# Block sums of w_out by transfers, and an earlier transpose of tokens, in a fused attention and feed-forward kernel

## The chip, the cores and the metric

The kernel runs on one core of one Trainium2 chip. The metric is the device time of one execution in microseconds; the time before is the median of three runs. A core has five engines with queues of their own: TensorE (PE; its weight loads are listed as PEld), VectorE (DVE), ScalarE (ACT), GpSimd (POOL) and SyncE (SP, which only issues transfers here). Transfers (DMA) are issued from an engine's queue and carried by 16 DMA engines. An engine works through its instructions in program order; one that waits holds up all that stand behind it.

## What is computed

There are two stages. For each of 8 batches and 8 heads, tokens `x` (512 x 64) and states (32 x 64) read one another by softmax attention. The 544 resulting rows of each batch, with 512 features, go through a feed-forward network with a leaky ReLU. Inputs and output are float32.

```python
B, H, S, Ns, D = (8, 8, 512, 32, 64)
scores = scale * np.matmul(x, state.transpose(0, 1, 3, 2))
a = softmax(scores)                       # over the 32 states
xread = np.matmul(a, state)
scores2 = scale * np.matmul(state, x.transpose(0, 1, 3, 2))
a2 = softmax(scores2)                     # over the 512 tokens
sread = np.matmul(a2, x)
rows = concatenate([xread, sread])        # (B * 544) x 512
h = rows @ w_in                           # 512 -> 2048
out = np.maximum(0.01 * h, h) @ w_out     # 2048 -> 512
```

(`softmax` and `rows` stand here for the few lines that the reference has in their place.)

## The kernel before

**Stages of a batch.** The 512 tokens of a batch are cast from `xl` (float32, one buffer) to `xb` (bf16, four buffers) and transposed to `xT` (two buffers). TensorE makes the scores `sc` from `xT` and the transposed states `st_t` (line 205). VectorE and ScalarE turn them into the probabilities `aT` (tokens over states) and `a2` (states over tokens). The product of states and `w_in` is made first, as `M` (line 326), so that the first layer of the tokens is one product of `M` and `aT` (line 347); ScalarE writes it through the leaky ReLU to `hT`. `a2` is transposed to `a2T`, and the states' reads `psr` (line 299) are made from `a2T` and `xb`; their feed-forward comes at the very end, for all batches together.

**Second layer.** Batches 0 and 1 go through `w_out` directly (`piece`, line 375). From batch 2 on, the product of `hT` and `w_out` is made by a scheme of the Strassen-Winograd kind: `hT` is seen as 2 x 2 blocks A, `w_out` as 2 x 2 blocks B11, B12, B21, B22, and seven block products are made in place of eight (class `Fast`; class `Batch` for tokens). The scheme needs four sums of blocks of A for each batch (`Fast.sums`, line 434, VectorE) and, once for the whole kernel, four sums of blocks of B, the tiles `tw[0]` to `tw[3]` (128 x 8 x 256 bf16, 512 KB each, in the buffers `xf0`, `xf1`, `x10` and `x11` that held early inputs). VectorE makes the sums of B in `weights_sum` (line 411), in batch 2. Product 6 uses `tw[1]`, 5 uses `tw[0]`, 7 uses `tw[2]`, and 4 uses `tw[3]`; they run in the order 1, 2, 6, 5, 7, 3, 4 as `units` of eight slices each. The outputs of a batch are put together by `join` (line 457, VectorE) and one addition on GpSimd (line 515), and stored in two transfers of 512 KB from SyncE (line 482).

**Order.** The order of instructions on every engine is the order of the program, written out by hand. Batch 1 and each batch from 2 on runs a loop of 16 steps `s`; a step makes one slice of the first layer and fills in slices of the second layer. In batch `b` the loop also prepares batches `b + 1` and `b + 2`:

- step 0: `load_x(b + 2)` (SyncE; it waits for the casts that read `xl` before) and the transpose `a2T` of batch `b` (SyncE)
- step 1: scores of batch `b + 1`, which need its `xT`; four casts of batch `b + 2` on GpSimd (line 105), which wait for `xl` and for the buffer of `xb` that batch `b - 2` had
- steps 3 and 8, batch 2 only: the sums of B; also in batch 2, the states' reads of batches 0, 1 and 2 in steps 4, 6 and 8, the load of the states of batches 4 to 7 (step 4) and their cast on GpSimd and transpose `st_t` (step 8)
- step 11: the transpose `xT` of batch `b + 2` on SyncE (`a_xt_dma`, line 189)

From batch 3 on, the second layer of the batch before is finished within this loop, and its two output transfers are put into SyncE's queue around steps 9 and 11, ahead of the transpose of step 11.

Of the kernel before, what the change touches and what calls it, by code (L numbers as in the profile page):

```python
# [10 lines left out]
B, H, S, D = 8, 8, 512, 64  # L11
# [16 lines left out]
def kernel(  # L28
# [240 lines left out]
    def a_exp2(a, g):  # L269
        if g == 0:  # L270
            a.e2 = att.tile([P, 2, S], BF16, name="e2", tag="e2")
            a.r2 = att.tile([P, 2], FP32, name="r2", tag="r2")
        nc.scalar.activation(  # L273
            out=a.e2[:, g], in_=a.sc[:, g, :], func=AF.Exp,
            bias=a.m2s[:, g:g + 1], scale=SCALE, accum_out=a.r2[:, g:g + 1],
        )
# [124 lines left out]
    def weights_open():  # L401
        for tag in ("xf0", "xf1", "x10", "x11"):
            tw.append(consts.tile([P, NM, HC], BF16, name=f"tw_{tag}", tag=tag))

    def weights_sum(dst):
        u, v, op = (
            (B12, B11, ALU.subtract), (B11, tw[2], ALU.subtract),
            (B22, B12, ALU.add), (tw[1], B21, ALU.add),
        )[dst]
        with nc.allow_low_precision(reason="operands of a product"):  # L410
            nc.vector.tensor_tensor(out=tw[dst][:], in0=u[:], in1=v[:], op=op)

    class Fast:

# [8 lines left out]
        def sums(self, n, m0=0, m1=NM, eng=None):  # L423
            A, S = self.A, self.S
            if n not in S:
                pool, tag, bufs = self.homes[n]
                S[n] = pool.tile([P, NM, self.q], BF16, name=f"su{n}", tag=tag, bufs=bufs)
            u, v, op = (
                (A[2, 1], A[2, 2], ALU.subtract), (S[0], A[1, 1], ALU.subtract),
                (A[2, 1], A[1, 1], ALU.subtract), (A[1, 2], S.get(1), ALU.add),  # L430
            )[n]
            ms = slice(m0, m1)
            with nc.allow_low_precision(reason="operands of a product"):
                (eng or nc.vector).tensor_tensor(out=S[n][:, ms], in0=u[:, ms], in1=v[:, ms], op=op)  # L434
# [19 lines left out]
            copy(t[:], bank)  # L454

        def join(self, dst, bank, n):
            nc.vector.tensor_tensor(out=dst, in0=bank, in1=self.sv[n][:], op=ALU.add)  # L457

    def rows_of(b):
        return out[b * SROW:b * SROW + S, :].rearrange("(p t) f -> t p f", t=NT)  # L460
# [2 lines left out]
    class Batch:  # L463
# [42 lines left out]
        def done(self, n, bank):  # L506
            f = self.f
            if n in (1, 6, 5, 7):
                f.save(n, bank)
            if n == 2:  # L510
                f.join(self.yo(0)[:, :, :HC], bank, 1)
                if self.b == B - 1:
                    self.out(0, slice(0, HC))
            elif n == 7:
                nc.gpsimd.tensor_tensor(  # L515
                    out=self.yo(1)[:, :, HC:], in0=f.sv[7][:], in1=f.sv[5][:], op=ALU.add
                )
                if self.b == B - 1:
                    self.out(1, slice(HC, DM), eng=nc.scalar)
            elif n == 3:  # L520
                f.join(self.yo(0)[:, :, HC:], bank, 6)
                self.out(0, slice(HC if self.b == B - 1 else 0, DM))
            elif n == 4:
                f.join(self.yo(1)[:, :, :HC], bank, 7)
                self.out(1)
# [257 lines left out]
    for s in range(16):  # L783
        ff1(a1, h1, s)
        if s % 2:
            pb, hT, i, jq = fill[s // 2]
            piece(pb, hT, i, jq, copy=VEC if s == 3 else SCA)
        if s == 4:
            a_scores(a2)
            m_evict(a2, 0, a_m(a2, 0, "big"), SCA)  # L790
            a_shift(a2)
            a_max2(a2)
        elif s == 7:
            a_exp(a2)
            a_open(att_of[3], 3)
            a_xt_dma(att_of[3])
        elif s in (9, 11):
            a_exp2(a2, s // 2 - 4)
            if s == 9:
                a_probs(a2)  # L800
            else:
                a_probs2(a2)
        elif s == 13:
            a_probs2(a1)
            a_a2t(a1)
            pm = [a_m(a2, 1, "big"), a_m(a2, 2, "sc")]
            m_evict(a2, 1, pm[0], VEC)
            m_evict(a2, 2, pm[1], SCA)
# [1 line left out]


    before = None
    weights_open()
    for b in range(2, B):
        hT = hpool.tile([P, 16, S], BF16, name="hT", tag="hT")
        a = att_of[b]
        nxt = att_of[b + 1] if b + 1 < B else None
        now = Batch(b, hT)
        std = []
        if b == 2:  # L820
            std = [(i, 3) for i in range(2)] + [(i, jq) for i in range(2, NT) for jq in range(4)]

        def fill(s):
            n = (PACE2 if b == 2 else PACE)[s]
            left = min(n, len(before.units)) if before else 0
            if left:
                before.run(left)
            if n > left:
                now.run(n - left)

        for s in range(16):
            if s == 11:
                fill(s)
            ff1(a, hT, s)
            if s == 0:
                if b + 2 < B:
                    load_x(b + 2, nc.sync)
                    open_xb(b + 2)
                a_a2t(a)
                if before:  # L840
                    for n in (0, 1):
                        before.f.sums(n, 4, 8)
            elif s == 1:
                if nxt is not None:
                    a_scores(nxt)
                m_evict(a, 3, a_m(a, 3, "big"), SCA)
                if nxt is not None:
                    a_shift(nxt)
                if b + 2 < B:
                    for h in range(0, H, 2):  # L850
                        cast_x(b + 2, h, h + 2, POO)
                if before:
                    before.f.sums(2, 4, 8)
            elif s == 3:
                if before:
                    before.f.sums(3)
                if nxt is not None:
                    a_max2(nxt)
                if b == 2:
                    weights_sum(0)  # L860
                    weights_sum(2)
            elif s == 4:
                if b == 2:
                    load_state(1)
                    a_sread(a0)
            elif s == 6:
                if b == 2:
                    a_sread(a1)
            elif s == 8:
                a_sread(a)  # L870
                if b == 2:
                    state_t(1)
                    weights_sum(1)
                    weights_sum(3)
            elif s == 11 and b + 2 < B:
                a_open(att_of[b + 2], b + 2)
                a_xt_dma(att_of[b + 2])
            elif s == 12:
                for n in range(3):
                    now.f.sums(n, 0, 4)  # L880
            if nxt is not None:
                if s == 5:
                    a_exp(nxt)
                elif s in (7, 8):
                    a_exp2(nxt, s - 7)
                    if s == 7:
                        a_probs(nxt)
                elif s == 11:
                    a_probs2(nxt)
                elif s in (12, 13):  # L890
                    SCA(nxt.M[:, s - 12, DM:2 * DM], pm1[:, s - 12, :])
            if std:
                i, jq = std.pop(0)
                piece(1, h1, i, jq)
            elif s != 11:
                fill(s)
            if s == 10 and nxt is not None:
                pm0 = a_m(nxt, 0, "big")
                pm1 = a_m(nxt, 1, "sc")
                pm2 = a_m(nxt, 2, "ph")  # L900
                for g, copy in enumerate((VEC, SCA)):
                    copy(nxt.M[:, g, 2 * DM:3 * DM], pm2[g][:])
                m_evict(nxt, 0, pm0, SCA)
        before = now
# [31 lines left out]
    for n, more in ((1, 2), (2, 2), (6, 1), (5, 1), (7, 1), (3, 0), (4, 0)):  # L936
        bank = v if n in (2, 5, 3) else u
        for m in range(NM):
            fs.unit(bank, n, m, first=n in (1, 2, 5, 4))
        if n in (1, 6, 5, 7):  # L940
            fs.save(n, bank)
        if n == 2:
            fs.join(ysb[0][:, :, :HC], bank, 1)
        elif n == 7:
            nc.gpsimd.tensor_tensor(
                out=ysb[1][:, :, HC:], in0=fs.sv[7][:], in1=fs.sv[5][:], op=ALU.add
            )
        elif n == 3:
            fs.join(ysb[0][:, :, HC:], bank, 6)
            out_s(0)  # L950
        elif n == 4:
            fs.join(ysb[1][:, :, :HC], bank, 7)
            out_s(1)
        before.run(more)
# [39 lines left out]
```

## Time and profile before

| | us |
|---|---|
| three runs | 211.01, 209.01, 211.02 (median 211.01) |
| profiled execution, its own time | 210.52 |
| its span | 208.7 |
| busy: TensorE, VectorE, ScalarE, GpSimd | 196.6, 144.3, 143.6, 41.4 |
| VectorE, four sums of B (line 411) | 1.21, 1.63, 1.22, 1.51 |
| transpose of tokens, issue to landing (6 of them) | 4.4 to 6.8, median 5.1 |
| transpose of `a2`, issue to landing (8) | 3.1 to 8.8, median 5.2 |
| load of `xl` from SyncE, 1 MB, issue to landing (5) | median 6.4 |

The span is that of the profiled instructions; the execution's own time has another 1.8 us around it. Times in the profile are microseconds from the start of the span. The profile names a tile by its name in the program without its number, so the four `tw` tiles appear as `tw_xf` (`tw[0]`, `tw[1]`) and `tw_x` (`tw[2]`, `tw[3]`), and the sums of A as `su`. The granted clock of TensorE is full throughout.

### The profile page before, as it was taken

The numbers are of one execution on the slowest core, as the hardware profiler recorded it, in microseconds if no ns is written. First come the engines' busy times: TensorE is split into PE (matmuls) and PEld (weight loads), VectorE is DVE, ScalarE is ACT, GpSimd is POOL, SyncE is SP. The second block draws the span as 40 slices with busy tenths as digits, with TensorE's granted clock in tenths as the row PEclk, the third lists the DMA queues.
The fourth block names the chain that finished last, engine by engine and source line by source line (L and its number), as shares of the span: only waits on it lengthen the run. The fifth ranks groups of instructions, "written<-read, shape, count | busy, mean of one in ns | idle before, by whom it ended". The sixth has DMA issues, their size and how long they took to land.

```text
span 208.7 us, 4393 instructions
## 1 busy us (share of the span) xinstructions
PE 196.6 (94%) x1779; PEld 126.4 (61%) x1804; DVE 144.3 (69%) x217; ACT 143.6 (69%) x276; POOL 41.4 (20%) x64
## 2 busy tenths in 40 slices
PE   6789999999999999999999999978999999999990
PEld 2443534443455567766776677645777677788880
DVE  1777589699699969976996699657966702462331
ACT  2459748688969897977797869765878864666210
POOL 8831002040053106200350054000020002000070
PEclk9999999999999999999999999999999999999999
DMA  5999993997655394059904960391025002210035
GB/s 177 229 207 285 220 268 93 208 302 146 182 156 168 96 243 91 3 201 201 155 0 180 229 152 0 137 194 27 0 104 151 0 3 100 100 53 0 3 84 167
DMA packets 38772, 27.74 MB, mean 133 GB/s; under 512 B 24352, under 2 KB 35744, under 8 KB 38752
## 3 DMA queue, kind: packets, MB, share of 16 engines
q1 hardware_dynamic: 33280, 20.39, 38.2%
q0 software_dynamic: 4912, 6.55, 15.3%
q10 hardware_dynamic: 560, 0.52, 1.0%
q8 instruction: 14, 0.23, 0.5%
q14 instruction: 6, 0.05, 0.1%
HBM read 17.30 MB, written 8.91 MB: 126 GB/s over the span
## 4 chain that ended last, share of the span: by engine, by line
PE 84%; DMA 6%; DVE 5%; ACT 2%; issue 1%; ACTq 0%
PE yq L445 34%; PE ph L347 20%; PE py L375 9%; PE pm L326 4%; PE ph L358 3%; PE pyw L375 3%; DMA xT<-xb 3%; DMA xf<-in_x_dram 2%; PE psr L299 2%; PE ph L691 2%; PE yu L445 2%; PE yv L445 1%; PE sc L205 1%; PE php L691 1%; DVE su L434 1%
## 5 line engine op out<-in xcount | busy, mean ns | idle before, releaser
L352 ACT ACTIVATE hT<-ph 128x512 bf16<-128x512 f32 x112 | 65.7, 603 | 22.5 <-PE ph L347 18.7
L347 PE MATMUL ph<-aT,M 128*128 128x512 bf16 x208 | 61.9, 379 | 0.8 <-ACT hT L352 0.5
L445 PEld LDWEIGHTS <-su 128*128 128x128 bf16 x416 | 39.9, 98 | 13.8 <-DVE su L434 1.2
L445 PEld LDWEIGHTS <-hT 128*128 128x128 bf16 x288 | 27.8, 98 | 12.7 <-issue 2.1
L105 POOL CAST xb<-xl 128x512 bf16<-128x512 f32 (+1 forms) x21 | 18.3, 910 | 62.8 <-DMA xl<-in_x_dram 49.5
L347 PEld LDWEIGHTS <-M 128*128 128x128 bf16 x224 | 21.7, 98 | 10.9 <-issue 1.7
L445 PE MATMUL yq<-tw_xf,su 128*128 128x256 bf16 x192 | 27.5, 273 | 0.3
L445 PE MATMUL yq<-w_out_bf,hT 128*128 128x256 bf16 x192 | 27.0, 273 | 0.1
L434 DVE TENSOR_TENSOR su<-hT 128x1024 bf16<-128x1024 bf16 x24 | 16.9, 705 | 11.0 <-ACT hT L352 11.0
L375 PE MATMUL py<-w_out_bf,hT 128*128 128x512 bf16 x91 | 23.4, 379 | 0.2
L375 PEld LDWEIGHTS <-hT 128*128 128x128 bf16 x128 | 11.9, 98 | 14.3 <-issue 1.3
L457 DVE TENSOR_TENSOR yo<-yq,sv 128x512 f32<-128x512 f32 x17 | 11.7, 685 | 11.6 <-PE yq L445 11.6
L515 POOL TENSOR_TENSOR yo<-sv,sv 128x512 f32<-128x512 f32 x6 | 7.6, 1268 | 47.6 <-ACT sv L454 43.7
L454 ACT COPY sv<-yq 128x512 f32<-128x512 f32 x24 | 14.0, 584 | 2.1 <-PE yq L445 1.4
L340 ACT CAST M<-pm 128x1024 bf16<-128x1024 f32 x13 | 13.2, 1014 | 2.9 <-PE pm L326 2.8
L445 PE MATMUL yq<-tw_x,su 128*128 128x256 bf16 x96 | 13.9, 273 | 0.0
L445 PE MATMUL yq<-w_out_bf,su 128*128 128x256 bf16 x96 | 13.1, 273 | 0.0
L445 PE MATMUL yq<-tw_x,hT 128*128 128x256 bf16 x88 | 12.1, 273 | 0.0
L215 DVE TRANSPOSE_TENSOR_REDUCE mrow<-sc 128x32 f32<-128x1024 f32 x7 | 8.7, 1245 | 4.1 <-PE sc L205 4.0
L273 ACT ACTIVATE e<-sc,mcols 128x512 bf16<-128x512 f32 x16 | 11.0, 693 | 0.1
L265 DVE TENSOR_REDUCE mcol<-sc 128x2 f32<-128x1024 f32 x8 | 9.7, 1214 | 0.0
L358 PE MATMUL ph<-sr_t,w_in_bf 128*128 128x256 bf16 x64 | 9.6, 273 | 0.0
(131 smaller groups left out, 256.1 us busy)
## 6 DMA issues: line engine op xcount, KB each, us to landing
xl<-in_x_dram SPq DMA_DIRECT2D x5, 1024.0 KB, 6.4
out_dram<-yo SPq DMA_DIRECT2D x10, 512.0 KB, 2.7
w_in_bf<-in_moe_w_in_dram POOLq DMA_DIRECT2D x4, 512.0 KB, 9.5
w_out_bf<-in_moe_w_out_dram POOLq DMA_DIRECT2D x4, 512.0 KB, 16.8
out_dram<-ysb SPq DMA_DIRECT2D x8, 256.0 KB, 4.6
xf<-in_x_dram SPq DMA_DIRECT2D x2, 512.0 KB, 5.4
x<-in_x_dram POOLq DMA_DIRECT2D x2, 512.0 KB, 13.6
xl<-in_x_dram POOLq DMA_DIRECT2D x1, 1024.0 KB, 18.6
```

The source lines that it names most:

```text
L105: copy(xs[b][:, :, h0:h1].rearrange("p t h d -> p h t d"), xl[b][:, h0:h1].rearrange("p h (t d) -> p h t d", t=NT),)
L265: nc.vector.tensor_reduce(out=m2[:], in_=a.sc[:], axis=AX.X, op=ALU.max, negate=True)
L273: nc.scalar.activation(out=a.e2[:, g], in_=a.sc[:, g, :], func=AF.Exp, bias=a.m2s[:, g:g + 1], scale=SCALE, accum_out=a.r2[:, g:g + 1],)
L340: copy(a.M[:, :, cols], pm[:])
L347: nc.tensor.matmul(ph[:], lhsT=a.M[:, g, P * j:P * (j + 1)], rhs=a.aT[:, g, :], start=(g == 0), stop=(g == 1),)
L352: nc.scalar.activation(out=hT[:, j, :], in_=ph[:], func=AF.Prelu, alpha=0.01)
L358: nc.tensor.matmul(ph[:, :n], lhsT=w_in_bf[:, k, P * j:P * (j + 1)], rhs=sr_t[:, k, :], start=(k == 0), stop=(k == NK - 1),)
L375: nc.tensor.matmul(y.py, lhsT=hT[:, j, P * i:P * (i + 1)], rhs=w_out_bf[:, j, :], start=(j == 0), stop=(j == 15),)
L434: (eng or nc.vector).tensor_tensor(out=S[n][:, ms], in0=u[:, ms], in1=v[:, ms], op=op)
L445: nc.tensor.matmul(bank[:, i, :], lhsT=lhs[:, m, P * i:P * (i + 1)], rhs=rhs[:, m, :], start=(first and m == 0 and (i == 0 or of is not No ...
L454: copy(t[:], bank)
L457: nc.vector.tensor_tensor(out=dst, in0=bank, in1=self.sv[n][:], op=ALU.add)
```

## The change

Three things are changed together.

The sums of B are made by transfers. In step 9 of the loop of batch 1, four plain transfers in SyncE's queue copy B11, B11, B12 and B21 into `tw[0]` to `tw[3]`. In batch 2, four transfers in GpSimd's queue add to them: `tw[2]` += B22 and `tw[0]` += B12 in step 0, `tw[1]` += `tw[2]` in step 3, and `tw[3]` += `tw[1]` in step 8. In program order on GpSimd, the first two stand ahead of the casts of step 1, the third behind these, and the fourth behind the cast of states of step 8. VectorE makes none.

Since a transfer only adds, signs change: `tw[0]` is B12 + B11 where it was B12 - B11, and `tw[1]` is B11 + B22 + B12 where it was B11 - (B22 + B12). The sum of A number 2 is negated, and product 6 (as saved in `sv[6]`) and the addition on GpSimd are subtracted where they were added.

The transpose of tokens for batch `b + 2` is issued in step 7 in place of step 11 from batch 3 on; in batch 2 it stays in step 11.

```diff
         for tag in ("xf0", "xf1", "x10", "x11"):
             tw.append(consts.tile([P, NM, HC], BF16, name=f"tw_{tag}", tag=tag))
+            nc.sync.dma_start(tw[-1][:], (B11, B11, B12, B21)[len(tw) - 1])
+
     def weights_sum(dst):
-        u, v, op = (
-            (B12, B11, ALU.subtract), (B11, tw[2], ALU.subtract),
-            (B22, B12, ALU.add), (tw[1], B21, ALU.add),
-        )[dst]
-        with nc.allow_low_precision(reason="operands of a product"):
-            nc.vector.tensor_tensor(out=tw[dst][:], in0=u[:], in1=v[:], op=op)
+        nc.gpsimd.dma_start(tw[dst][:], (B12, tw[2][:], B22, tw[1][:])[dst], accum_op=ALU.add)
...
-                (A[2, 1], A[1, 1], ALU.subtract), (A[1, 2], S.get(1), ALU.add),
+                (A[1, 1], A[2, 1], ALU.subtract), (A[1, 2], S.get(1), ALU.add),
...
         def join(self, dst, bank, n):
-            nc.vector.tensor_tensor(out=dst, in0=bank, in1=self.sv[n][:], op=ALU.add)
+            op = ALU.subtract if n == 6 else ALU.add
+            nc.vector.tensor_tensor(out=dst, in0=bank, in1=self.sv[n][:], op=op)
...
-                    out=self.yo(1)[:, :, HC:], in0=f.sv[7][:], in1=f.sv[5][:], op=ALU.add
+                    out=self.yo(1)[:, :, HC:], in0=f.sv[5][:], in1=f.sv[7][:], op=ALU.subtract
...
         elif s in (9, 11):
+            if s == 9:
+                weights_open()
...
-    weights_open()
     for b in range(2, B):
...
                 a_a2t(a)
+                if b == 2:
+                    weights_sum(2)
+                    weights_sum(0)
...
                 if b == 2:
-                    weights_sum(0)
-                    weights_sum(2)
+                    weights_sum(1)
...
                     state_t(1)
-                    weights_sum(1)
                     weights_sum(3)
-            elif s == 11 and b + 2 < B:
-                a_open(att_of[b + 2], b + 2)
-                a_xt_dma(att_of[b + 2])
...
+            if s == (11 if b == 2 else 7) and b + 2 < B:
+                a_open(att_of[b + 2], b + 2)
+                a_xt_dma(att_of[b + 2])
```

The addition in the states' own feed-forward at the end (line 946) is changed to a subtraction in the same way.

More of the change, by code (lines that the diff above doesn't have):

```diff
@@ L945 @@
             nc.gpsimd.tensor_tensor(
-                out=ysb[1][:, :, HC:], in0=fs.sv[7][:], in1=fs.sv[5][:], op=ALU.add
+                out=ysb[1][:, :, HC:], in0=fs.sv[5][:], in1=fs.sv[7][:], op=ALU.subtract
             )
```

## The prediction

> **What bounds the kernel now.** I read the page's engine totals and slices first, then the waits, the chain of waits, and the instructions in order of time on SyncE's queue, TensorE, GpSimd and VectorE.
>
> ```profile
> PE 196.6 (94%) x1779; PEld 126.4 (61%) x1804; DVE 144.3 (69%) x217; ACT 143.6 (69%) x276; POOL 41.4 (20%) x64
> PE   6789999999999999999999999978999999999990
> ```
>
> TensorE is busy for 196.6 of 208.7 us and has 12.1 us left. The second line (40 slices of 5.2 us) shows where: the start, the last slice, and one dip at slices 26 and 27. VectorE has 31% to spare, so taking work from it helps only where TensorE waits for it.
>
> ```profile
> PE sc L205 <- DMA xT<-xb: 2.2, 1, 2.2
> ```
>
> In TensorE's own waits (us in all, times, longest) the dip is one wait of 2.2 us, for a transpose of tokens; the next longest, 1.2 us, is at the start. In the chain of waits the same place reads (start, us, what):
>
> ```profile
> 134.84 6.84 DMA xT<-xb
> ...
> 141.72 0.41 PE sc L205 x8
> ```
>
> This is the transpose for batch 7, issued in step 11 of batch 5. Earlier ones land after 5.1 us, at 91.94 + 5.1 = 97.0 and 113.22 + 5.1 = 118.3, and their scores run at 97.13 and 118.31: nearly no slack there either. They are issued late because SyncE's queue goes in order and stands behind two output transfers that wait for `yo`. The median of three runs is 211.01 us with one run at 209.01; one such stall could be that difference, which a single trace can't show.
>
> Now SyncE's queue around the block sums (start, us):
>
> ```profile
> 46.70 2.67 SPq L189 DMA_TRANSPOSE xT<-xb  x1
> 52.33 1.23 SPq L291 DMA_TRANSPOSE a2T<-a  x1
> 53.61 0.57 SPq L99 DMA_DIRECT2D xl<-in_x_dram  x1
> 59.75 1.24 SPq L291 DMA_TRANSPOSE a2T<-a  x1
> ...
> 70.53 2.81 SPq L189 DMA_TRANSPOSE xT<-xb  x1
> ```
>
> and who needs them on TensorE:
>
> ```profile
> 65.20 0.63 PE L299 MATMUL psr<-a2T,xb 128*128 128x64 bf16 x16
> ...
> 75.99 0.41 PE L205 MATMUL sc<-xT,st_t 64*32 64x512 bf16 x8
> ...
> 76.55 1.05 PE L445 MATMUL yq<-tw_xf,su 128*128 128x256 bf16 x8
> ```
>
> The `a2T` issued at 59.75 lands after 3.1 us at 62.85 and is needed at 65.20: 2.35 us of slack. The `xT` issued at 70.53 lands after 5.2 us at 75.7 and is needed at 75.99: 0.3 us. The first use of a block sum is 76.55 (`tw[1]`), then `tw[2]` at 81.78 and `tw[3]` at 87.47.
>
> **The transpose moved to step 7 (batches 3 to 5).** It goes ahead of both output transfers. It then waits only for GpSimd's casts: in batch 5 these end at 122.62 + 3.74 = 126.4, so even with the slow landing of 6.84 it is there at 133.2, for a need at 139.5. On the queue it takes 3.5 us, to 129.9; the output behind it starts at 131.05, so nothing is pushed. In batch 3 the casts end at 83.6 and the output comes at 88.85: again clear. The next `xl` and `a2T` go out earlier. Worth 2.2 us, the whole stall; bounds 0 (a run without it) and 2.2. In batch 2 nothing moves.
>
> **VectorE's sums taken away.** 1.21 + 1.63 + 1.22 + 1.51 = 5.57 us, at 60.5 to 63.2 and 66.9 to 69.7. TensorE waits for VectorE nowhere between 56 and 76, so zero; it can't lose, and at most about 0.4 us of small waits on `su` later could go. GpSimd's four casts beside them took 4.34 us, against 3.14 in batch 4; I take 3.3. The three changed signs cost nothing: the same instruction with another operation.
>
> **Four plain transfers (step 9 of the batch-1 loop).** They wait for nothing recent and go out behind the `xT` of 46.70, from 49.4, 0.5 us each, done before the `a2T` of 52.33. Each moves 512 KB in pieces of 512 bytes. The trace has no such transfer, but rows on both sides of that size (window, share of the engines' time, GB/s at the end):
>
> ```profile
> 56.00:58.00 2.00, 2.00 (x11) 0.88 (x9) 1.93 (x3) 1.40 (x4) 0.00 (x0) 1.00 1.03 368
> 73.00:75.00 2.00, 2.00 (x16) 1.36 (x14) 0.47 (x2) 1.96 (x4) 0.00 (x0) 1.00 1.12 207
> 25.00:26.00 1.00, 1.00 (x13) 0.71 (x11) 0.52 (x1) 0.00 (x0) 0.00 (x0) 1.00 1.22 204
> ```
>
> The first is `xl` in 1 KB pieces, the second transposes within SBUF in smaller ones, the third the converting loads that GpSimd issued. So 1.4 us (368) to 2.5 us (207) each; by pieces, 1 KB takes 1024 x 16 / 368 = 45 ns on one engine, and half of it 23 to 25 ns, 64 pieces per engine: 1.6 us. I take that, 6.4 in all. The engines are free from 50.7 (the `xT` done) and now stay busy to 57.1.
>
> **Four adding transfers (GpSimd's queue).** One reads two blocks and writes one. Low end 1.4 us, a plain copy; high end 104 ns a piece, the mean of GpSimd's queue (15.3% of 16 engines' span over 4912 packets), 6.7 us. I take two reads of 512 bytes as one piece of 1 KB, 45 ns, 3 us; the converting loads' 204 GB/s gives 2.5. GpSimd issues one in 0.8 to 0.9 us, as it did its loads. The first waits for the third plain transfer, which lands at about 50.7 + 4.8 + 0.8 = 56.3; both are out at 58, and GpSimd had nothing to do before 59.94, so this wait alone blocks nobody. But their 6 us of traffic meets SyncE's.
>
> That meeting is the price. At 57.1 SyncE's queue still owes `a2T` (1.4 us of the engines' time, 0.71 of the 2 us from 53) and `xl` (3.2 us, the shares from 55 to 59 added), then the second `a2T` (1.4). How SyncE's transfers fare beside a full queue of GpSimd's, the DMA issues show (KB each, us to landing):
>
> ```profile
> stf<-in_state_dram SPq DMA_DIRECT2D x8, 32.0 KB, 2.2
> ...
> stf<-in_state_dram SPq DMA_DIRECT2D x8, 16.0 KB, 6.2
> ```
>
> Small loads of states landed after 6.2 us at the start, between GpSimd's weight loads, and twice as large ones after 2.2 us later, without them. So SyncE's queue has no precedence, and I let the two share evenly. The first `a2T` is through at 58.5 and lands near 59.5, needed at 62.15: no wait. `xl` takes 2 x 3.2 us and ends at 64.9 in place of 58.6; the `a2T` behind it has the rest of the adds beside it, ends near 67.4 and lands near 68.3. Needed at 65.20: **TensorE waits 3.1 us**.
>
> The Trainium skill ("DMA: Bandwidth & Descriptors", Why small descriptors are slow (HBM only)) says that transfers within SBUF are spared what small pieces cost, and its section Where 436 GB/s comes from lets them run at 435 GB/s, 1.2 us a plain transfer. By that page, an estimate, the adds begin at 57 and the second `a2T` lands near 65.5, the wait shrinks to 0.3 us and the time to 209.1. The transposes within SBUF at 207 GB/s above speak against it; it counts with the rival in which nothing is late.
>
> What else is late: casts from 65.6 to 68.9 in place of 64.3; then, new in GpSimd's order, the third add (0.9 us), so the cast of states ends at 70.9 in place of 68.6; the transpose of states (68.65 before), an output and `xT` follow at about 72.8, landing at 78, 2.0 us after 75.99. TensorE is by then 3.1 us late already, so this lies inside it. The third add, issued at 69.8, lands at about 75.5, before 76.55 + 3.1; the fourth waits for it on GpSimd, whose next work is at 79.86, and lands by 81 for 87.47.
>
> Sum: 210.52 (the profiled execution: span 208.7 and 1.8 around it) - 2.2 + 3.1 = 211.4. The median lies 0.5 above that execution: **211.9 us**.
>
> **The rivals.** *Nothing is late.* The adds run at 1.4 us, or SyncE's queue is hardly slowed: without sharing, `xl` ends at 61.7 and `a2T` lands at 64.0, within its slack, and the casts end at 66, so `st_t` and `xT` slip by under 0.5 us. For it: all engines are idle from 51 to 53 and near 59 to 60. Against: three transfers in a row have to stay on time with 0.3 us left on the last. Time: 210.5 - 2.2 + 0.5 = 208.8.
>
> *The adds are slow, and the change ends slower.* At 6.7 us each, with plain ones at 2.5, the first two adds keep the engines to about 74; `xl` ends at 68 to 70, `a2T` lands at 72 to 73, 7.5 us after 65.20. The third add, which waits for the first and stands behind the casts, lands near 82 for a need at 76.55, 5.5 us, inside the same delay. Time: 210.5 - 2.2 + 7.5 + 0.5 = 216.3. Between the forecast (3 us an add, a wait of 3.1) and this, the wait passes 4.3 us, the gain of 2.2 and 1% of the time besides, at about 4 us an add: there it decides. For it: 104 ns is what that queue showed; against: that was beside the whole start-up load.
>
> *The early transpose doesn't do it*, because SyncE waits for late casts at step 7. It would give back the 2.2 us, 211 with nothing late and 214 with the wait of 3.1. The casts end 13 us before the need in batch 5, so it has no chance of its own.
>
> **How the numbers follow.** About 1% is what a measurement of this kernel can tell from no change: 208.9 to 213.1. Forecast (wait of 1.5 to 5 us, 210.3 to 213.8): 0.45, of which 0.27 within 1% and 0.18 above. Nothing late: 0.30, of which 0.27 faster by over 1% (208.8 is just that) and 0.03 not quite. Slow adds: 0.25, all slower. Together 0.27 faster, 0.30 within, 0.43 slower. The forecast's own range is 210.3 to 213.8; one that holds 8 in 10 has to take in both rivals, 208.8 and 216.3, each with a few tenths for the median's spread: 208.4 to 216.5.
>
> **What would show it.** In TensorE's waits, `sc <- xT` of batch 6 is gone, and a wait `psr <- a2T` of some 3 us stands near 65, in batch 2. The plain transfers land in 1.6 us steps from 52 to 58; the adds last 3 us; GpSimd's casts of batch 2 start near 65.6. Wrong if the casts still start at 60, if a wait for `tw` shows at 76, or if stalls appear in batches 3 to 5.

## The result and the profile after

The changed kernel takes 223.06 us (median of 4 runs, 220.55 to 223.80), the kernel before 210.91 beside it: a ratio of 1.056 (95% interval 1.049 to 1.063). Medians here and below are of all runs, while ratios leave out those over 1.5% above the fastest of their kernel (213.31 us of the kernel before, 222.93 of `adds_states_early`, and 342.8 of `both_early`, at a granted clock of 0.56). The change makes the kernel slower by 12 us; the forecast was 211.9, the top of its range 216.5. The profiled execution took 220.55 us with a span of 218.8, 10.1 more than before. The page's totals and the granted clock in 40 slices (5.5 us each):

```profile
PE 199.6 (91%) x1779; PEld 127.3 (58%) x1804; DVE 137.6 (63%) x213; ACT 144.0 (66%) x276; POOL 41.0 (19%) x68
PEclk9999999999998579999999999999999999999999
```

VectorE is 6.7 us less busy, and no gain from it shows. TensorE is 3 us busier with the same instructions; its clock fell in slices 12 to 14, counted from 0. Its longest waits (us in all, times, longest):

```profile
PE psr L299 <- DMA a2T<-a: 7.9, 1, 7.9
PE sc L205 <- DMA xT<-xb: 1.7, 2, 1.3
```

The 2.2 us for `xT` in batch 6 are gone, as forecast. The wait of `psr` for `a2T` is where it was forecast, near 65, and 7.9 us long in place of 3.1. In the chain of waits (start, us, what) a second transfer follows it:

```profile
59.90 13.42 DMA a2T<-a
...
82.15 6.38 DMA xT<-xb
88.53 0.04 issue
88.57 0.41 PE sc L205 x8
```

The scores of batch 4 start at 88.57, at 75.99 before: 12.6 us late. From there on nothing more is lost; the span is 10.1 longer, which is 12.6 less the 2.2 of batch 6 and a few tenths. So these scores are the place that counts, and both transfers in the chain come late. SyncE's queue (start, us to issue):

```profile
49.82 1.41 SPq L406 DMA_DIRECT2D tw_xf<-w_out_bf  x2
51.33 2.87 SPq L406 DMA_DIRECT2D tw_x<-w_out_bf  x2
54.29 3.60 SPq L291 DMA_TRANSPOSE a2T<-a  x1
57.94 1.50 SPq L99 DMA_DIRECT2D xl<-in_x_dram  x1
59.90 5.76 SPq L291 DMA_TRANSPOSE a2T<-a  x1
...
67.08 8.44 SPq L169 DMA_DIRECT2D stf<-in_state_dram  x8
...
79.49 1.19 SPq L176 DMA_TRANSPOSE st_t<-stb  x1
...
82.15 4.50 SPq L189 DMA_TRANSPOSE xT<-xb  x1
```

and GpSimd (start, us, idle before and what ended it):

```profile
57.80 1.58 POOL L409 DMA_DIRECT2D tw_x<-w_out_bf  x1 [11.01 <-DMA tw_x<-w_out_bf]
58.71 2.27 POOL L409 DMA_DIRECT2D tw_xf<-w_out_bf  x1
69.74 2.29 POOL L105 CAST xb<-xl 128x512 bf16<-128x512 f32 x4 [8.77 <-DMA xl<-in_x_dram]
71.97 0.86 POOL L409 DMA_DIRECT2D tw_xf<-tw_x  x1
78.84 0.62 POOL L175 CAST stb<-stf 128x512 bf16<-128x512 f32 x1 [6.01 <-DMA out_dram<-ysb]
```

The issues themselves have become long while the transfers' engines are full: the eight small loads of states take 8.4 us to issue, where before, with the cast that needs them, they read:

```profile
62.15 3.86 SPq L169 DMA_DIRECT2D stf<-in_state_dram  x8
...
67.53 1.10 POOL L175 CAST stb<-stf 128x512 bf16<-128x512 f32 x1 [3.24 <-DMA stf<-in_state_dram]
```

The adds land after 10.2, 14.3, 6.0 and 6.4 us, the plain transfers after 3.6 to some 8.5. The casts, forecast for 65.6, start at 69.7, and the cast of states at 78.8 where it was at 67.5.

### The profile page after: what moved, and what is told of

Same layout as the page of the kernel before. It is cut to its first block, busy times and chain, and to the rows that moved or that the text cites. A ratio compares the mean times of both kernels' runs of the same rounds, so it can differ in the third digit from the quotient of the medians.

```text
span 218.8 us, 4403 instructions
## 1 busy us (share of the span) xinstructions
PE 199.6 (91%) x1779; PEld 127.3 (58%) x1804; DVE 137.6 (63%) x213; ACT 144.0 (66%) x276; POOL 41.0 (19%) x68
## 4 chain that ended last, share of the span: by engine, by line
PE 65%; DMA 25%; DVE 3%; POOL 2%; issue 1%; ACT 1%; SPq 0%; POOLq 0%; ACTq 0%
PE yq L443 32%; PE ph L347 17%; DMA xl<-in_x_dram 9%; DMA a2T<-a 6%; DMA xT<-xb 5%; DMA w_in_bf<-in_moe_w_in_dram 5%; PE py L375 4%; PE ph L358 3%; PE pm L326 3%; PE psr L299 2%; PE yu L443 2%; PE yv L443 1%; PE sc L205 1%; POOL w_in_bf L118 1%; DVE su L432 1%
## 5 line engine op out<-in xcount | busy, mean ns | idle before, releaser
L347 PE MATMUL ph<-aT,M 128*128 128x512 bf16 x208 | 62.9, 384 | 0.8 <-ACT hT L352 0.5
L375 PE MATMUL py<-w_out_bf,hT 128*128 128x512 bf16 x91 | 25.0, 399 | 0.4 <-issue 0.2
L105 POOL CAST xb<-xl 128x512 bf16<-128x512 f32 (+1 forms) x21 | 13.4, 682 | 54.4 <-DMA xl<-in_x_dram 54.4
L432 DVE TENSOR_TENSOR su<-hT 128x1024 bf16<-128x1024 bf16 x24 | 16.4, 685 | 11.0 <-ACT hT L352 11.0
L375 PEld LDWEIGHTS <-hT 128*128 128x128 bf16 x128 | 12.3, 101 | 15.2 <-issue 2.9
L457 DVE TENSOR_TENSOR yo<-yq,sv 128x512 f32<-128x512 f32 x17 | 11.6, 685 | 11.6 <-PE yq L443 11.6
L904 DVE CAST M<-pm 128x512 bf16<-128x512 f32 x5 | 3.5, 692 | 20.7 <-PE pm L326 20.7
L340 ACT CAST M<-pm 128x1024 bf16<-128x1024 f32 x13 | 13.2, 1014 | 2.5 <-PE pm L326 2.5
L299 PE MATMUL psr<-a2T,xb 128*128 128x64 bf16 x128 | 5.4, 199 | 8.1 <-DMA a2T<-a 7.9
```

Source lines behind the costliest of these rows:

```text
L105: copy(xs[b][:, :, h0:h1].rearrange("p t h d -> p h t d"), xl[b][:, h0:h1].rearrange("p h (t d) -> p h t d", t=NT),)
L299: nc.tensor.matmul(ps[:, k, :, :], lhsT=a.xb[:, i, 2 * k:2 * k + 2, :].rearrange("p h d -> p (h d)"), rhs=a.a2T[:, :, i, NS * k:NS * (k + 1)],
L340: copy(a.M[:, :, cols], pm[:])
L347: nc.tensor.matmul(ph[:], lhsT=a.M[:, g, P * j:P * (j + 1)], rhs=a.aT[:, g, :], start=(g == 0), stop=(g == 1),)
L375: nc.tensor.matmul(y.py, lhsT=hT[:, j, P * i:P * (i + 1)], rhs=w_out_bf[:, j, :], start=(j == 0), stop=(j == 15),)
```

## The experiments

All runs are set beside the kernel before on the same chip, whose median lay between 210.8 and 212.0.

**The two parts of the change apart.** `xt7_only` is the kernel before with this part of the diff alone:

```diff
-            elif s == 11 and b + 2 < B:
+            if s == (11 if b == 2 else 7) and b + 2 < B:
```

> The kernel before with the transpose of tokens at step 7 from batch 3 on, and the sums of B still on VectorE. Theory (the move is good by itself and the sums cost everything): the wait of 2.2 us of sc for xT in batch 6 is gone, nothing else changes, 208.7 us. Rival (the move does nothing or pushes the outputs): 210.9 us or more.

Measured: 208.22 us (208.15 to 208.67), a ratio of 0.985 (0.981 to 0.989). In TensorE's instructions the scores of batch 7, at 141.72 before after 2.2 us of waiting, now run at:

```profile
139.45 0.41 PE L205 MATMUL sc<-xT,st_t 64*32 64x512 bf16 x8
```

The move is worth what was forecast: 2.3 us between the two profiled executions, 2.6 between the medians. This version is faster than both kernels. `sums_only` is the changed kernel with `if s == 11 and b + 2 < B`.

> The changed kernel with the transpose of tokens back at step 11 in all batches. Theory: the wait of psr for a2T near 65 stays at some 8 us and the wait of sc for xT in a late batch comes back, about 2 us above the changed kernel's 223, so 225 us. Rival (the move has part in the loss): below 222 us.

Measured: 222.83 us, ratio 1.056 (1.048 to 1.063). The sums carry the whole loss. The late stall did not come back, against the theory: its `xT` of batch 7 was issued at 148.55 for scores at 153.8, and landed in time. So the 2 us of the move are there only beside the kernel before.

**Plain transfers alone, adds alone.** `plain_only` is `xt7_only` with the four plain transfers; VectorE then makes the sums over them.

```diff
+            nc.sync.dma_start(tw[-1][:], (B11, B11, B12, B21)[len(tw) - 1])
...
+            if s == 9:
+                weights_open()
```

> The kernel before with the transpose at step 7 and with the four plain transfers at step 9 of batch 1; VectorE then makes the sums as before and overwrites what they brought, so there are no adds. Theory (it takes plain transfers and adds together, the adds being the larger part): plain transfers of 1.9 us each end at 58.3, a2T of batch 2 lands near 65.3, a wait of psr of at most 0.5 us, 208.7 to 209.5 us. Rival (what stands in SyncE's queue ahead of xl and a2T is enough by itself): a wait of 4 us or more, 214 us or more.

Measured: 209.90 us, ratio 0.993 (0.990 to 0.997); 1.7 us more than `xt7_only` and 0.4 above the theory's range. `psr` does not wait for `a2T`; TensorE's longest wait stands at the scores of batch 4:

```profile
PE sc L205 <- DMA xT<-xb: 1.5, 2, 1.2
```

Plain transfers alone nearly fit in. For adds alone, `adds_only` set `tw` to zero by memsets.

```diff
-            nc.sync.dma_start(tw[-1][:], (B11, B11, B12, B21)[len(tw) - 1])
+            if len(tw) in (2, 4):
+                nc.gpsimd.memset(tw[-1][:], 0.0)
...
+                    nc.vector.memset(tw[2][:], 0.0)
+                    nc.vector.memset(tw[0][:], 0.0)
```

> The changed kernel without the four plain transfers: tw is set to zero by memsets in their place (VectorE sets tw[0] and tw[2] after the subtraction of step 1, so that the adds go out near 59.5), and the adds are as in the change. Left out: the blocks B11, B12 and B21 that the plain transfers bring. Theory: xl is through before the adds begin, a2T of batch 2 shares with them and lands at 64 to 66, a wait of psr of 0 to 1 us; the third add holds up GpSimd, so sc of batch 4 waits some 2 us for xT; 209 to 212 us. Rival (adds alone do it): a wait of psr of 5 us or more, 215 us or more.

Measured: 223.81 us, but the run tells little of the adds: beside the two memsets on GpSimd (46.53 to 50.08) two instructions of VectorE became long, and what stands behind came 2 to 4 us late (VectorE, start, us):

```profile
46.33 3.78 DVE L267 TENSOR_SCALAR mcols<-mcol 128x2 f32<-128x2 f32 x1
46.52 3.59 DVE L237 TRANSPOSE_TENSOR_REDUCE r<-e 128x32 f32<-128x1024 bf16 x1
```

(0.29 and 1.23 us before). `psr` did not wait for `a2T` in it; the scores waited 9.5 us for `xT`. `adds_clean` has VectorE copy the blocks into `tw` in batch 2 in place of both.

```diff
-            nc.sync.dma_start(tw[-1][:], (B11, B11, B12, B21)[len(tw) - 1])
...
+                    for n in (2, 0, 1, 3):
+                        VEC(tw[n][:], (B11, B11, B12, B21)[n])
+                    weights_sum(2)
+                    weights_sum(0)
```

> The changed kernel with the four plain transfers replaced by four copies on VectorE (after the subtraction of step 1 in batch 2); the adds follow them, near 60 and 61, and all else is as changed. Theory (traffic: each add takes some 4.5 us of all 16 engines, and the third holds up GpSimd's cast of states): a2T of batch 2 lands near 65 to 67, a wait of psr of 0 to 2 us; the loads and the cast of states are late, so sc of batch 4 waits 4 to 7 us for xT; with the lost clock 214 to 220 us. Rival (plain transfers and adds are needed together): no wait over 1.5 us, 208.5 to 210.5 us.

Measured: 220.60 us, ratio 1.041 (1.034 to 1.047). `psr` does not wait at all, and yet the scores of batch 4 start 11.4 us late, against 12.6 with the change:

```profile
PE sc L205 <- DMA xT<-xb: 11.8, 2, 11.3
```

So the adds without the plain transfers make most of the loss, and the wait for `a2T` is not needed for it. The wait is longer than the theory's 4 to 7 us. `plain_for_adds` keeps all eight transfers and makes the adds plain ones.

```diff
-        nc.gpsimd.dma_start(tw[dst][:], (B12, tw[2][:], B22, tw[1][:])[dst], accum_op=ALU.add)
+        nc.gpsimd.dma_start(tw[dst][:], (B12, tw[2][:], B22, tw[1][:])[dst])
```

> The changed kernel with the four adds turned into plain transfers of the same blocks, from the same queue at the same places, with the same waits. Left out: the additions, so tw holds single blocks. Theory (what an add costs over a plain transfer is engine time, 4.5 us against 1.9): the first two take 5 us less, the wait of psr falls from 7.9 to some 2 or 3 us, the clock stays, 212 to 215 us. Rival (waits and order in GpSimd's queue, not traffic): within 1% of the changed kernel's 223 us.

Measured: 216.20 us, ratio 1.021 (1.014 to 1.028). The adding costs some 7 us over plain transfers of the same blocks, so the rival of waits and order alone is out. The time is still above the theory's 212 to 215, and the wait of `psr` above its 2 to 3:

```profile
PE psr L299 <- DMA a2T<-a: 5.3, 2, 4.8
```

**The low clock.** During the wait the clock goes down to half, and it stays there for some 6 us behind it (window; the last three columns are clock, share of the transfers' engines and GB/s):

```profile
66.00:74.00 8.00, 0.55 (x11) 0.58 (x12) 0.63 (x1) 0.21 (x1) 3.09 (x5) 0.70 1.25 237
74.00:78.50 4.50, 4.28 (x18) 1.78 (x17) 0.00 (x0) 1.90 (x5) 0.00 (x0) 0.50 1.01 227
```

The stretch from the reads of batch 2 to the first `yq` takes 5.9 us where it took 3.1. `warm_wait` fills the wait with products.

```diff
+                if b == 2:
+                    spin(36, "big")
                 a_sread(a)
```

> The changed kernel with 36 products of 512 columns on a zero tile (7.8 us) ahead of the reads of the states of batch 2, so that TensorE is busy where it waited. Added: these products, whose result nobody uses. Theory (2.9 us of the loss is the lower clock that follows the wait): the granted clock stays at 1.00 from 66 to 80, the next 6 us run at full speed, 219.5 to 221 us. Rival (the slower products after the wait have to do with the transfers): no gain, 223 us or more.

Measured: 224.01 us, ratio 1.059 (1.052 to 1.065). The clock stayed full through that stretch, as meant (TensorE, start, us):

```profile
65.44 7.93 PE L132 MATMUL pspin<-idle 128*128 128x512 bf16 x36
73.43 0.63 PE L299 MATMUL psr<-a2T,xb 128*128 128x64 bf16 x16
...
89.58 0.63 PE L205 MATMUL sc<-xT,st_t 64*32 64x512 bf16 x8 [5.30 <-DMA xT<-xb]
```

and TensorE then waited 5.3 us for `xT`. That is the rival's outcome: the 2.9 us of low clock cost nothing by themselves, for the wait of 7.9 us and the low clock lie under the lateness of `xT`.

**Other orders.** If the scores of batch 4 set the time, what comes before them in the queues may be at fault. `a2t_first` issues `a2T` of batch 2 ahead of `xl`, into a buffer of its own; `states_early` loads, casts and transposes the states in batch 1; `both_early` does both; `adds_states_early` is `adds_clean` with the states in batch 1.

```diff
             if s == 0:
+                if b == 2:
+                    a_a2t(a)
...
     load_x(3, nc.sync)
+    load_state(1)
...
             a_xt_dma(att_of[3])
+            state_t(1)
```

> The changed kernel with the transpose a2T of batch 2 ahead of the load of xl in SyncE's queue, into a buffer of its own. Theory (two chains are late under the same traffic, and the later one, loads of states - their cast - their transpose - xT of batch 4, sets the time): the wait of psr is under 1 us, the wait of sc for xT grows to 9 to 12 us, and the time stays at 221 to 225 us. Rival (the wait of psr for a2T is the loss): 211 to 215 us.

> The changed kernel with the loads of the states of batches 4 to 7, their cast and their transpose moved into batch 1, before the transfers for the sums. Theory (two chains): xT of batch 4 lands by 82, the wait of sc is gone, but the wait of psr of 6 to 8 us and the low clock after it stay, 219.5 to 222 us. Rival (the chain of the states alone is the loss): 211 to 215 us.

> The changed kernel with both moves of the other two runs, a2T of batch 2 first and the states in batch 1. Theory (both chains are relieved; left is xl, its casts and xT of batch 4 beside the adds): no wait of psr over 1 us, a wait of sc of 2 to 5 us, 211 to 215 us. Rival (the transfers' total sets the time, whatever the order): 219 us or more.

> The kernel with copies on VectorE and adds by transfers, with the states moved into batch 1. Theory: with the states out of the way the adds only slow xT of batch 4 and its casts, a wait of sc of 0 to 3 us in place of 11.3, 208.5 to 212 us. Rival (the adds' traffic delays xT itself): a wait of sc of 6 us or more, 215 us or more.

Measured: 221.48 us (ratio 1.044, 1.039 to 1.049); 220.70 us, of four runs at 218.66, 218.91, 222.49 and 224.44, with no interval; 224.37 us (1.058, 1.053 to 1.063); 214.43 us (1.011, 1.006 to 1.016). The first two times are near what the theory of two late chains forecast, but the traces are not. `a2t_first` took 5.3 us off the wait for `a2T` and left 2.6, where under 1 was forecast; the scores then waited 5.8 us, where 9 to 12 were forecast, and started only 1.0 us earlier than with the change. In `states_early` `xT` landed at 86.6, where 82 was forecast. The third came out against the theory: with both chains relieved, nothing was gained. The fourth lies between its theory and its rival.

**What an add costs by itself.** `alone` puts one plain transfer and two adds into batch 6.

```diff
+            if s == 8 and b == 6:
+                q = xpool.tile([P, 2, NM, HC], BF16, name="xq", tag="xl", bufs=1)
+                nc.sync.dma_start(q[:, 0], B11)
+                nc.gpsimd.dma_start(q[:, 0], B12, accum_op=ALU.add)
+                nc.gpsimd.dma_start(q[:, 0], tw[2][:], accum_op=ALU.add)
```

> The kernel before with the transpose at step 7, and in batch 6, where the transfers' engines have nothing else to do, one plain transfer of B11 on SyncE's queue, one add of B12 in pieces of 512 bytes and one add of tw[2] in pieces of 4 KB on GpSimd's queue, one after another into a tile that nobody reads. Theory: plain 3.2 to 3.6 us to landing, of which 1.9 of engine time; the first add 6 to 6.5 us, of which 4.5; the second less, 5 us. Rival (adds are as fast as plain ones when nothing else runs): under 4.5 us. The time stays at 208.2 to 209 us.

Measured: 208.58 us in one run; to landing 3.8 us for the plain one, 8.0 for the first add, beside which two outputs went out, and 5.3 for the second. In one execution of `adds_states_early`, of 222.9 us where the others took 213.7 to 214.5, a transpose beside an add took 19.7 us to land. `pairs` sends three pairs at once in the quiet last part; both of a pair wait for a small memset.

```diff
+                nc.gpsimd.dma_start(q[:, 0], B12, accum_op=ALU.add)
+                q_transpose()
...
+        if j == 5:
+            nc.gpsimd.dma_start(q[:, 0], B21)
+            q_transpose()
+        elif j == 12:
+            nc.gpsimd.dma_start(q[:, 0], B12, accum_op=ALU.add)
+            nc.sync.dma_start(q[:, 1], B11)
```

> The kernel before with the transpose at step 7, and in the quiet last stretch three pairs of transfers that start together, into a tile that nobody reads: an add of 512 KB on GpSimd's queue beside a transpose of 512 KB on SyncE's; a plain transfer on GpSimd's queue beside the same transpose; an add on GpSimd's queue beside a plain transfer on SyncE's. Theory 1 (fair shares of engine time, 4.2 us an add, 2.5 to 2.9 a transpose, 1.9 a plain one): the pairs are through after 8.5, 6 and 7.5 us to landing. Theory 2 (an add and a transpose hurt each other beyond their shares): the first pair takes 12 us or more, the other two as in theory 1.

Measured, 207.95 us in one run; to landing: add 8.5 and transpose 4.5; plain 6.7 and transpose 7.1; add 7.6 and plain 3.8. Fair shares said 8.5, 6 and 7.5. In the last pair one sees each kind run (windows, share and GB/s at the end):

```profile
192.00:194.00 2.00, 2.00 (x21) 1.80 (x19) 0.68 (x2) 0.07 (x1) 0.31 (x1) 1.00 0.89 247
194.00:198.00 4.00, 4.00 (x40) 3.58 (x38) 0.42 (x1) 1.53 (x4) 1.43 (x2) 1.00 1.15 132
```

Mostly the plain one moves first, 512 KB in some 1.9 us; then the add alone keeps all 16 engines full for 4 us at 132 GB/s. `both_plain` is `both_early` with plain transfers for the adds; `both_again` and `adds_again` are `both_early` and `adds_states_early` once more. In the texts that follow, theory 2 is that an add and a transpose hurt each other beyond their shares.

> The changed kernel with a2T of batch 2 first and the states in batch 1 (as in the run both_early), and the four adds turned into plain transfers from the same queue. Left out: the additions. Theory 2 (adds beside transposes): no such slow stretch, a wait of sc of at most 3 us, 209 to 213 us. Rival (whatever is sent in that stretch, the total sets the time): 216 us or more, as in the run plain_for_adds.

> The same kernel as both_early, for a profile at full clock. Theory 2: sc of batch 4 waits 8 us or more for xT, which is issued beside an add and takes 12 us or more to land, at under 150 GB/s; 221 to 225 us. Theory 1: xT lands within 8 us of its issue, which itself comes late behind xl and its casts.

> The same kernel as adds_states_early, for a profile of its usual run. Theory 2: xT of batch 4, issued at 69.4 beside the third add, takes 8 to 12 us to land, and sc waits 3 to 5 us; 213.5 to 214.6 us. Theory 1: xT lands within 8 us, sc waits under 2 us, and the loss is elsewhere.

Measured: 214.32 us (ratio 1.013, 1.006 to 1.021), between the two theories; 223.31 us; 214.24 us. In `both_again` `xT` was issued at 75.40, took 13.2 us to land, and the scores started at 88.69. In `adds_again` it was issued at 69.55, took 11.0, and the scores waited 4.1, as theory 2 had it; in `both_again` they waited 6.7, where it had 8 or more. The last add of GpSimd's queue went out when `xT` was about to land or had landed (`adds_again`, then `both_again`):

```profile
79.06 0.85 POOL L408 DMA_DIRECT2D tw_x<-tw_xf  x1 [8.17 <-issue]
```

```profile
88.72 0.85 POOL L410 DMA_DIRECT2D tw_x<-tw_xf  x1 [10.91 <-DMA tw_xf<-tw_x]
```

## Why the prediction was wrong

**What held.** The bound and the stall were read rightly: the move of the transpose is worth its 2.2 us beside the kernel before, and no gain shows from VectorE's sums, 5.57 us, though no run takes them away alone. A part of the mechanism was right too: the adds meet SyncE's transfers on the same 16 engines, GpSimd's queue has its share, `psr` waits for `a2T` at the place named, the third add holds up the cast of states, and no wait for a `tw` shows.

**The step that failed** is "What else is late", which let the lateness of the scores of batch 4, 2.0 us, lie inside the wait for `a2T`. It is the other way round: the scores are 12.6 us late, and in `adds_clean` 11.4 without any wait for `a2T`. That step delayed the cast of states by GpSimd's order (the casts and the third add) and by nothing else; the adds' traffic beside the loads of states, the transpose of states and `xT` was put at nothing, although the forecast shows a row in which such loads took 6.2 us to land beside GpSimd's queue. Measured, these loads landed after 6.8 us in place of 2.2 and were all issued only at 75.5. The cast behind them ended at 79.5 where 70.9 was forecast, `xT` went out at 82.15 where 72.8 was, and landed after 6.4 us where 5.2 was. So 11.6 us of the lateness were there when `xT` was issued, 70.53 before.

The sum of the forecast followed one transfer, `a2T`, and the two adds beside it; it did not count the third and fourth add against `xT`, the last of SyncE's transfers that TensorE needs. A sum over the profile before comes near it. Its engines for transfers, from the end of one `xT` to the landing of the next (length first, share next to last):

```profile
50.70:53.00 2.30, 2.25 (x24) 0.90 (x10) 2.19 (x8) 1.78 (x3) 0.00 (x0) 1.00 0.00 0
53.00:59.00 6.00, 6.00 (x42) 2.50 (x41) 4.24 (x5) 4.50 (x8) 0.00 (x0) 1.00 0.77 221
59.00:61.00 2.00, 1.95 (x24) 1.15 (x23) 1.97 (x3) 1.00 (x3) 1.06 (x2) 1.00 0.02 3
61.00:68.00 7.00, 6.95 (x61) 3.68 (x60) 6.86 (x8) 6.50 (x15) 3.76 (x4) 1.00 0.69 186
68.00:70.00 2.00, 2.00 (x34) 1.05 (x33) 1.75 (x3) 1.14 (x3) 0.62 (x1) 1.00 0.06 12
70.00:75.70 5.70, 5.65 (x39) 3.60 (x38) 4.05 (x9) 5.64 (x11) 0.00 (x0) 1.00 0.80 181
```

Length times share gives 14.2 us busy of 25, so 10.8 us are free. The change sends four plain transfers of 1.9 us and, ahead of `xT`, four adds of 4: 23.6 us. 23.6 - 10.8 = 12.8 us late; measured 12.6. The 4 us were measured after the forecast, and the sum was made then. By the forecast's own sizes (1.6 and 3) the same sum gives 18.4 - 10.8 = 7.6, and with the 2.2 off and the half microsecond to the median 216.4, near its upper rival. The forecast had 3.1 of this lateness: by this sum it left out 4.5 us in the accounting and 5.2 by the sizes.

The sum can be held against the other orders by the start of the scores of batch 4. Of the added transfers, those are counted that went out ahead of `xT`. The fourth add, or the plain transfer in its place, is not counted where it went out less than 2 us before `xT` landed (`adds_again`, `both_plain`, `states_early`) or after (`both_again`):

| kernel | ahead of `xT`, us | by the sum | measured |
|---|---|---|---|
| before | 0 | 75.99 | 75.99 |
| plain_only | 7.6 | 75.99 | 78.18 |
| both_plain | 13.3 | 78.5 | 82.45 |
| adds_clean | 16.0 | 81.2 | 87.42 |
| adds_only | 16.0 | 81.2 | 89.95 |
| adds_again | 12.0 | 77.2 | 80.58 |
| plain_for_adds | 15.2 | 80.4 | 85.03 |
| changed | 23.6 | 88.8 | 88.57 |
| sums_only | 23.6 | 88.8 | 88.14 |
| warm_wait | 23.6 | 88.8 | 89.58 |
| a2t_first | 23.6 | 88.8 | 87.55 |
| states_early | 19.6 | 84.8 | 86.67 |
| both_again | 19.6 | 84.8 | 88.69 |

Where all four plain transfers and all four adds go ahead of `xT`, the sum holds within 1.3 us. Everywhere else, but for the kernel before, the scores come 1.9 to 6.2 us later than it says, beside `adds_only`, which is late from its memsets. So the transfers' total by itself is not shown to set the time, not for `both_early` either: its time is the rival's, 219 us or more, but `both_again` sent only seven of the eight ahead of `xT` and was 3.9 us later than their sum. And the match of 0.2 us for the change itself is in part luck, for its own trace has a stretch in which the transfers' engines stand nearly still, which the sum has no place for:

```profile
78.00:80.00 2.00, 2.00 (x10) 1.00 (x8) 0.00 (x0) 0.96 (x2) 1.16 (x2) 0.63 0.05 19
```

SyncE issues nothing from 76.0 to 79.49; then the transpose of states goes out, right behind the end of their cast. So two things make `xT` late: the chain of the states, which comes late behind the full engines, and the adds beside `xT` itself. With the states out of the way, in `adds_again`, `xT` goes out at 69.55, a microsecond earlier than before, and still lands 4.9 us late, after 11.0 us in place of 5.2. Four adds with the states behind them make 11.4 us of lateness, nearly that of all eight transfers, and four plain ones 2.2. Shown is that the adds make most of the lateness, and that it stands at the scores of batch 4. How it divides between engine time and order is not shown. The Trainium skill ("DMA: Bandwidth & Descriptors", Issuing engines are not separate DMA queues) says that transfers from all queues run on the same 16 engines and interleave. The traces agree: adds from GpSimd's queue, without the plain transfers, make the scores that need SyncE's `xT` 11.4 us late.

**The sizes.** Plain: 1.9 us against 1.6 taken; the four were to be issued before the `a2T` of 52.33, but took SyncE until 54.2. Add: 4 us against 3 taken, between the bounds of 1.4 and 6.7; the converting loads at 204 GB/s, which the forecast had as its third row, were no guide, for an add moves 132. The wait for `a2T` was 7.9 us against 3.1.

**The rivals.** "The adds are slow" was nearest in its end, 216.3, and its 7.5 us for `a2T` is close to the 7.9 measured. But it came to this with adds of 6.7 us, where they took 4, and it priced the third add at `tw`, where nothing waited: the closeness is luck. "Nothing is late" is refuted by the waits for `a2T` and `xT`. The Trainium skill's rate within SBUF ("DMA: Bandwidth & Descriptors", Where 436 GB/s comes from), 435 GB/s, was counted with that rival. The trace of `pairs` does not agree: a plain transfer takes 1.9 us, 276 GB/s, and the measurement decides.

**Not forecast at all:** the low clock after the wait, 2.9 us in the trace, though by `warm_wait` it did not add to the time.

**Open.** That an add and a transpose hurt each other beyond their shares is not shown by `pairs`; but `both_again` has stretches of 80 to 98 GB/s from 84 to 86 with both in flight, and the one execution with 19.7 us is unexplained. Nor do the runs say why `plain_for_adds` is 2.6 us later than `both_plain`, or why moving the states ahead takes 6.8 us off the lateness of the adds alone and at most 1.9 off that of all eight.

## What to carry to other kernels

Before work is moved from an engine to transfers, add up the free time of the transfers' engines between the last moment it can start and the last transfer that somebody needs, and set the full engine time of all that is added against it; here, where it didn't fit, no order tried brought the scores forward by more than 1.9 us. Such a sum is a first estimate only, for where less was sent the order and the chains behind a full queue counted for up to 6 us more. So follow as well what is queued behind the new transfers, to the last one that somebody needs. A transfer's cost is the time that it keeps the engines, and the deadline that counts is the last one in the queue, not the first that is late. Work taken off an engine that nobody waited for bought nothing that shows here to set against that.

## What the runs showed of the hardware

- An add within SBUF of 512 KB keeps all 16 engines for about 4 us (132 GB/s), a plain transfer of the same bytes for 1.9 (`pairs`).
- In the profile of the change the granted clock averages 0.81 between 68 and 70 and 0.50 from 70 to 78, after TensorE had stopped at 65.6, and is full again some 6 us after it resumed at 73.45. The 0.81 puts the fall near 69.2, 3.6 us after the stop. The Trainium skill ("TensorE: Matmul & The Clock Gate", Part 1: The HAM clock gate) gives half rate after about 3.4 us of idling, and as much of work before full rate. The first agrees here; the second took longer. In `a2t_first` a wait of only 2.6 us was followed by 0.50 from 69 to 71, which does not agree, and the measurement decides.
- Beside two GpSimd memsets of 128 x 2048 bf16 (1.81 us each) a VectorE instruction of 0.29 us took 3.78 (`adds_only`).
- With the transfers' engines full, SyncE needs longer to issue: 8.4 us for eight loads of states in place of 3.9, and 5.8 for a transpose in place of 1.2.
